# Second mlp's first product by seven block products for each pair of row tiles

## The chip, the cores and the metric

The kernel runs on one core of a Trainium2 chip. The metric is the device time of one execution in microseconds (us). Engines are named as in the profile: PE is the matrix engine (PEld its weight loads), DVE, ACT and POOL are the three elementwise engines, SP issues the DMAs. L559 is line 559 of the kernel.

## The reference, cut to what matters

```
scores  = x @ state^T / 8            # attention of 512 tokens x 32 states, 8 heads of 64
out     = concat(softmax(scores) @ state, softmax(scores^T) @ x)
x       = out as 4352 rows of 512
x       = (sigmoid(x @ w_gate) * (x @ w_val)) @ w_out        # first mlp, 512 -> 1536 -> 512
h       = x @ w_in                                           # second mlp, 512 -> 1024
s       = h * softmax(h)
y       = layernorm(s) * g_ln @ w_out2                       # 1024 -> 512
```

The changed part is `h = x @ w_in`: for a tile of 128 rows, 512 inputs in 4 blocks of 128 and 1024 outputs in two halves of 512.

## The kernel before

The 4352 rows are 8 blocks of 512 (one for each batch) and one block of 256 (the read of the state side, SREAD), that is 34 tiles of 128 rows. All wide products keep each operand as a high and a low part: `mm3` (L136 to L139) issues three matmuls, high by high (L137), low by high (L138), high by low (L139). The parts are made by a *split*: the high part by an ACT copy (`hi_of`, L128), the low part by a subtraction on DVE (`lo_of`, L134) or POOL. 

**First mlp.** Its instructions stand in program order on each engine. The blocks run one after the other, each in 12 passes (c = 0 to 11) of 24 matmuls: 6 into the bank gps (gate), 6 into the bank vps (value), 12 that add pass c-1 to the block's output in acc0 to acc3. Around them, in one pass: ACT takes the sigmoid of gps (L559, called sigma(c) below; the gate products of pass c+1 write the same bank, so they wait for it), DVE multiplies it with vps (L563), ACT and DVE split the result (gh L128, gl L569), and split the next state weights (mh L128, ml L134). In SREAD and in the last block a weight converter (`conv`) runs beside this, one step in each pass from c = 2 on: ACT L194 and L195, DVE L202, L205, L212, POOL L222 turn a 128 x 512 piece of weights from DRAM into f32, and ACT L233 and DVE L234 split the piece of the pass before. In the last block these are the pieces of w_out2, and POOL has only L222 to do.

**Second mlp.** From L995 on the order is made by a scheduler from a model of the engines, out of program order. Tile i: 2 halves by 4 k by 3 = 24 matmuls (`h2_mm`, L616 to L622), row maxima (DVE L625), exponential (ACT L632), product with h (DVE L635), layer norm (DVE L636, L637; ACT L640 applies it), then a transpose: DVE L674 by 32 x 32, a write to DRAM and four reads back (SP L675, L677), and a split of what comes back (ACT L128 into woh9, woh10, woh11 and xe2; POOL L686). 24 matmuls with w_out2 into att0 or att1 follow (`out2`, L688 to L694), and a scaled store (ACT L699, SP). Inputs of later blocks lie in DRAM, are read by `y_load` and split by `y_split` (L604 to L609: 4 ACT, 4 POOL instructions of 128 x 512 a block). Blocks come in the order 7, 0, SREAD, 1 to 6.

## Time and profile before

| | us |
|---|---|
| median of 3 runs | 1138.1 (1137.03 to 1147.5) |
| the profiled execution | 1136.54 |
| its span, first to last instruction | 1134.6 |
| PE busy in the span | 1101.0 (97%) |
| DVE, ACT, POOL busy | 691.8, 556.5, 301.7 |
| mean granted clock of PE | 0.997 of full speed |
| last block of the first mlp (12 passes) | about 685 to 752 |
| second mlp, from its first to its last first product | about 752 to 1110 |

The profiled execution is 1.56 us (0.14%) below the median. 1.94 us of it lie outside the span. The page's share of an engine is an average over stages that differ; the views by window and the timelines in the section on rows show the two stages that the change touches. In a timeline a row is start, duration, engine, line, operation, output and inputs, shapes, and in brackets how long the engine had been idle before and what ended that. Ends of matmuls are modelled.

### The profile page before, as it was taken

The numbers are of one execution on the slowest core, as the hardware profiler recorded it, in microseconds if no ns is written. First come the engines' busy times: TensorE is split into PE (matmuls) and PEld (weight loads), VectorE is DVE, ScalarE is ACT, GpSimd is POOL, SyncE is SP. The second block draws the span as 40 slices with busy tenths as digits, with TensorE's granted clock in tenths as the row PEclk, the third lists the DMA queues.
The fourth block names the chain that finished last, engine by engine and source line by source line (L and its number), as shares of the span: only waits on it lengthen the run. The fifth ranks groups of instructions, "written<-read, shape, count | busy, mean of one in ns | idle before, by whom it ended". The sixth has DMA issues, their size and how long they took to land.

```text
span 1134.6 us, 15718 instructions
## 1 busy us (share of the span) xinstructions
PE 1101.0 (97%) x5591; PEld 876.0 (77%) x5591; DVE 691.8 (61%) x1279; ACT 556.5 (49%) x1036; POOL 301.7 (27%) x301
## 2 busy tenths in 40 slices
PE   7878899999999999999999999999999999999998
PEld 5555567778878778778778998888888888888787
DVE  6999865467465475564674465758465555555462
ACT  6766445545444555443554454654453443434333
POOL 2776633300000000000000151233353443424231
PEclk9999999999999999999999999999999999999999
DMA  8763130331440421622412334424454434333331
GB/s 234 255 204 98 26 89 1 80 87 35 119 120 20 124 58 38 171 69 64 98 31 77 131 113 130 121 72 162 138 169 132 154 121 148 121 112 121 112 124 53
DMA packets 139550, 122.87 MB, mean 108 GB/s; under 512 B 70992, under 2 KB 111184, under 8 KB 139472
## 3 DMA queue, kind: packets, MB, share of 16 engines
q1 hardware_dynamic: 139472, 121.87, 36.4%
q8 instruction: 44, 0.72, 0.3%
q14 instruction: 34, 0.28, 0.1%
HBM read 78.32 MB, written 43.52 MB: 107 GB/s over the span
## 4 chain that ended last, share of the span: by engine, by line
PE 61%; DMA 13%; DVE 12%; ACT 5%; issue 4%; SPq 3%; POOL 1%; ACTq 0%; POOLq 0%; DVEq 0%
PE acc L137 9%; PE acc L139 9%; PE acc L138 9%; DMA ut<-usp 6%; DMA usp<-ub 6%; PE gps L137 4%; PE gps L138 4%; PE gps L139 4%; PE vps L137 4%; PE vps L139 4%; PE vps L138 4%; SPq L677 2%; PE att L139 2%; PE att L137 2%; PE att L138 2%
## 5 line engine op out<-in xcount | busy, mean ns | idle before, releaser
L137 PE MATMUL acc<-gh,woh 128*128 128x512 f32 (+1 forms) x432 | 168.0, 389 | 0.0
L138 PE MATMUL acc<-gl,woh 128*128 128x512 f32 (+1 forms) x432 | 164.1, 380 | 1.7 <-POOL gl L569 1.3
L139 PE MATMUL acc<-gh,wol 128*128 128x512 f32 (+1 forms) x432 | 164.0, 380 | 0.0
L563 DVE TENSOR_TENSOR sg<-vps,sg 128x512 f32<-128x512 f32 (+1 forms) x108 | 71.1, 659 | 150.5 <-PE vps L139 136.6
L559 ACT ACTIVATE sg<-gps 128x512 f32<-128x512 f32 (+1 forms) x108 | 61.8, 572 | 160.7 <-PE gps L139 156.2
L686 POOL TENSOR_TENSOR wol<-ut,woh 128x512 fp32r<-128x512 f32 x48 | 61.7, 1301 | 193.1 <-ACT woh L128 176.7
L137 PEld LDWEIGHTS acc<-gh,woh 128*128 128x128 f32 x432 | 81.5, 189 | 31.0 <-issue 15.6
L138 PEld LDWEIGHTS acc<-gl,woh 128*128 128x128 f32 x432 | 81.6, 189 | 17.7 <-POOL gl L569 2.2
L139 PEld LDWEIGHTS acc<-gh,wol 128*128 128x128 f32 x432 | 81.4, 188 | 16.0
L128 ACT ACTIVATE woh<-ut 128x512 fp32r<-128x512 f32 x48 | 28.6, 627 | 122.4 <-DMA ut<-usp 121.9
L128 ACT ACTIVATE gh<-sg 128x512 fp32r<-128x512 f32 (+1 forms) x101 | 60.5, 599 | 49.3 <-DVE sg L563 49.3
L137 PE MATMUL gps<-ah,mh 128*128 128x512 f32 x192 | 76.1, 396 | 5.2 <-DVE ml L134 4.0
L139 PE MATMUL att<-woh,wol 128*128 128x512 f32 (+1 forms) x204 | 79.5, 390 | 0.6 <-POOL wol L686 0.6
L137 PE MATMUL att<-woh,woh 128*128 128x512 f32 (+1 forms) x204 | 79.5, 390 | 0.0
L138 PE MATMUL att<-wol,woh 128*128 128x512 f32 (+1 forms) x204 | 79.1, 388 | 0.0
L134 DVE TENSOR_TENSOR ml<-gps,mh 64x512 fp32r<-64x512 f32 (+2 forms) x57 | 38.7, 678 | 63.1 <-ACT stg L128 51.0
L222 POOL TENSOR_TENSOR tt<-tt,xn 128x512 int32<-128x512 int32 x16 | 20.9, 1306 | 211.5 <-PE vps L139 153.8
L137 PE MATMUL vps<-ah,mh 128*128 128x512 f32 x192 | 75.4, 393 | 1.1 <-DVE ml L134 1.1
L138 PE MATMUL gps<-al,mh 128*128 128x512 f32 x192 | 75.6, 394 | 0.9 <-DVE al L134 0.9
L128 ACT ACTIVATE mh<-gps 64x512 fp32r<-64x512 f32 (+2 forms) x53 | 31.3, 590 | 91.6 <-PE gps L139 60.5
L139 PE MATMUL gps<-ah,ml 128*128 128x512 f32 x192 | 75.5, 393 | 0.0
L255 POOL MEMSET xtr<- 32x256 f32 x18 | 5.4, 302 | 262.2 <-PE att L323 261.5
(288 smaller groups left out, 2750.0 us busy)
## 6 DMA issues: line engine op xcount, KB each, us to landing
usp<-ub SPq DMA_DIRECT2D x32, 512.0 KB, 2.6
ut<-usp SPq DMA_DIRECT2D x128, 128.0 KB, 2.9
msp<-stg SPq DMA_DIRECT2D x72, 128.0 KB, 2.3
stg<-msp SPq DMA_DIRECT2D x36, 256.0 KB, 2.9
xn<-in_x_dram SPq DMA_DIRECT2D x15, 512.0 KB, 5.2
e2t<-in_x_dram SPq DMA_DIRECT2D x96, 64.0 KB, 2.6
stge<-in_moe_w_out_dram SPq DMA_DIRECT2D x10, 512.0 KB, 4.4
stge<-in_moe_w_gate_dram SPq DMA_DIRECT2D x9, 512.0 KB, 5.1
```

Of the source, the lines that this page charges most:

```text
L128: return act(dst, src, AF.Copy)
L134: return vec.tensor_tensor(out=dst, in0=src, in1=r(hi), op=ALU.subtract)
L137: mm(o, lh, rh, start=start, stop=False)
L138: mm(o, lh, rl, start=False, stop=False)
L139: return mm(o, ll, rh, start=False, stop=stop)
L222: pool.tensor_tensor(out=ti, in0=ti, in1=lo, op=ALU.add)
L255: pool.memset(s[:, :, 64 * (1 - i):64 * (1 - i) + 64], 0.0)
L559: act(sg[c % 2][:, 0:n], gps[:, 0:n], AF.Sigmoid)
L563: vec.tensor_tensor(out=g, in0=vps[:, 0:n], in1=g, op=ALU.mult)
L677: nc.sync.dma_start(out=w[32 * b:32 * b + 32].rearrange("p (a e) -> p a e", a=4), in_=d.rearrange("(a j) (b e) -> b j a e", a=4, b=4)[b],)
L686: pool.tensor_tensor(out=lv, in0=wv[:, 4 * q:4 * q + 4], in1=r(hv), op=ALU.subtract)
```

## The change

The 30 tiles of all blocks but the first (15 pairs) get `h` by seven products of a 128 x 256 block of x with a 256 x 512 block of w_in, in Winograd's form of Strassen's scheme. A pair has two row tiles (A1x, A2x) and two column halves of x; w_in has blocks B11 to B22. With S1 = A21 + A22, S2 = S1 - A11, S3 = A11 - A21, S4 = A12 - S2 and T1 = B12 - B11, T2 = B22 - T1, T3 = B22 - B12, T4 = B21 - T2 (`y_pair_ops`, `w_pair_ops`), `product` issues 2 x 3 matmuls for one of P1 to P7: 42 for a pair instead of 48. P6 and P7 are added onto P1 in PSUM; three ACT copies (L1116, L1121, L1123) and three DVE additions (`plus`) for each pair form the four quarters of h from them. Pairs alternate between the banks acc0, acc1, acc2 and acc3, gps, vps. The products' order is 1, 2, 5, 6, 3, 7, then out2 of tile i-2, then 4, then out2 of tile i-1.

The sums of inputs are made in `y_pair_ops`: 7 splits and 4 sums a block, 7 ACT and 11 POOL instructions instead of 4 and 4. The sums of weights are made once, in the last block of the first mlp, two steps after each pass (`w_steps`): 8 joins of high and low part, 8 differences and 8 splits, each a 128 x 512 instruction on POOL, and for each split one on ACT. Buffers are merged to make room (tt and ee are now wa, xtr and e2t wb); the out buffers are 2 instead of 4. The first block's 4 tiles are done as before, and the first mlp before its last block is as it was. The diff, cut to its core:

```diff
-    xtr = [f32t(f"xtr{i}", S) for i in range(2)]
-    tt = [f32t(f"tt{g}", S) for g in range(2)]
-    ee = [f32t(f"ee{g}", S) for g in range(2)]
-    e2t = [f32t(f"e2t{g}", S) for g in range(2)]
+    wa, wb = f32t("wa", 4, S), f32t("wb", 4, S)
+    tt, ee = [[wa[:, 2 * n + g] for g in range(2)] for n in range(2)]
+    xtr, e2t = [[wb[:, 2 * n + g] for g in range(2)] for n in range(2)]
...
-    stt = [f32t(f"stt{i}", 4, 64) for i in range(2)]
+    sttb = f32t("stt", 2, 4, 64)
+    stt = [sttb[:, i] for i in range(2)]
...
-        sbx = (ctx if p < 3 else x_late).enter_context(tc.tile_pool(name=f"sbx{p}", bufs=1, side="right"))
+        sbx = (ctx if p < 2 else x_late).enter_context(tc.tile_pool(name=f"sbx{p}", bufs=1, side="right"))
...
-    ob = sg + spill[0:2]
+    ob = sg
...
+    p1, u2 = spill[0:2]
+    p5 = sttb.rearrange("p i j n -> p (i j n)")
+    ys, ts = [], {}
+    A11, A12, A22, S1, S2, S3, S4 = range(7)
+    prod = {1: (A11, "B11"), 2: (A12, "B21"), 3: (S4, "B22"), 4: (A22, "T4"), 5: (S1, "T1"), 6: (S2, "T2"), 7: (S3, "T3")}
 
...
+    def y_pair_ops(q):
+        m = S if order[q] < B else SR
+        v = yf[q % 2][:, :, 0:m].rearrange("p (c k) (t r s) -> p c k t r s", c=2, r=2, s=P)
+        a = {(i + 1, c + 1): v[:, c, :, :, i, :] for i in range(2) for c in range(2)}
+        def split(n, src):
+            h, l = [x[:, 0:2 * (m // 2)].rearrange("p (k t s) -> p k t s", k=2, s=P) for x in ys[q % 2][n]]
+            def f():
+                hi_of(h, src)
+                pool.tensor_tensor(out=l, in0=src, in1=r(h), op=ALU.subtract)
+            return f
+        def add(dst, x, y, op):
+            return lambda: pool.tensor_tensor(out=dst, in0=x, in1=y, op=op)
+        return [
+            split(A11, a[1, 1]), split(A12, a[1, 2]), split(A22, a[2, 2]),
+            add(a[2, 2], a[2, 1], a[2, 2], ALU.add), split(S1, a[2, 2]),
+            add(a[2, 1], a[1, 1], a[2, 1], ALU.subtract), split(S3, a[2, 1]),
+            add(a[1, 1], a[2, 2], a[1, 1], ALU.subtract), split(S2, a[1, 1]),
+            add(a[1, 2], a[1, 2], a[1, 1], ALU.subtract), split(S4, a[1, 2]),
+        ]
+    def w_pair_ops(bf):
+        steps = []
+        for k in range(2):
+            b = {n: x for n, x in zip(("B11", "B12", "B21", "B22"), bf[4 * k:4 * k + 4])}
+            def join(n):
+                h, l = win(k + 2 * (n[1] == "2"), int(n[2]) - 1)
+                return lambda: pool.tensor_tensor(out=b[n], in0=r(h), in1=r(l), op=ALU.add)
+            def sub(o, x, y):
+                return lambda: pool.tensor_tensor(out=b[o], in0=b[x], in1=b[y], op=ALU.subtract)
+            def split(n, x):
+                h, l = ts[n, k]
+                def f():
+                    hi_of(h, b[x])
+                    pool.tensor_tensor(out=l, in0=b[x], in1=r(h), op=ALU.subtract)
+                return f
+            steps += [
+                join("B11"), join("B12"), sub("B11", "B12", "B11"), split("T1", "B11"),
+                join("B22"), sub("B12", "B22", "B12"), split("T3", "B12"),
+                sub("B22", "B22", "B11"), split("T2", "B22"),
+                join("B21"), sub("B21", "B21", "B22"), split("T4", "B21"),
+            ]
+        return steps
 
...
+    def banks(i):
+        return ([acc[0], acc[1], acc[2]], [acc[3], gps, vps])[i // 2 % 2]
 
     def h2_out(i, f):
-        return acc[2 * (i % 2) + f]
+        if tiles[i][0] == 0:
+            return acc[2 * (i % 2) + f]
+        a, b, c = banks(i)
+        return ((b, c), (a, p5))[i % 2][f]
+    def product(i, n, o, start, stop):
+        q, b, t = tiles[i]
+        x, w = prod[n]
+        h, l = ys[q % 2][x]
+        m = (S if b < B else SR) // 2
+        for k in range(2):
+            sl = slice(m * k + P * (t // 2), m * k + P * (t // 2) + P)
+            w1, w2 = win(k + 2 * (w[1] == "2"), int(w[2]) - 1) if w[0] == "B" else ts[w, k]
+            mm3(o, h[:, sl], l[:, sl], w1, w2, start and k == 0, stop and k == 1, skip_group_check=True)
...
+    def plus(o, x, y):
+        vec.tensor_tensor(out=o, in0=x, in1=y, op=ALU.add)
 
...
-        return (woh[9 + n], wol[9 + n]) if n < 3 else (wpart(xe, 2, 0), wpart(xo, 2, 0))
+        return (woh[9 + n], wol[9 + n]) if n < 3 else [x.rearrange("p k n -> p (k n)") for x in (sth, stl)]
...
+                x_late.close()
+                sbt = ctx.enter_context(tc.tile_pool(name="sbt", bufs=1, side="right"))
+                for w in ("T1", "T2", "T3", "T4"):
+                    for k in range(2):
+                        ts[w, k] = [sbt.tile([P, 512], F32R, name=f"{w}{e}{k}") for e in "hl"]
+                more = [[sbt.tile([P, 512], F32R, name=f"ys{i}{e}") for e in "hl"] for i in range(6)]
+                ys += [[*zip(yh[i], yl[i]), *more[3 * i:3 * i + 3]] for i in range(2)]
+                bf_pool = ExitStack()
+                sbf = bf_pool.enter_context(tc.tile_pool(name="sbf", bufs=1, side="right"))
+                w_steps = w_pair_ops([sbf.tile([P, 512], F32, name=f"bf{i}") for i in range(8)])
...
+                if last:
+                    for _ in range(2):
+                        w_steps.pop(0)()
...
+    for i in range(len(first), nt, 2):
+        q, b, t = tiles[i]
+        if t == 0 and q + 1 < len(order):
+            ops = y_pair_ops(q + 1)
+        o, v, w = banks(i)
+        end = i + 2 == nt
+        product(i, 1, o, True, False)
+        act(p1, o, AF.Copy)
+        product(i, 2, v, True, True)
+        plus(v, v, p1)
+        h_max(i, 0)
+        product(i, 5, w, True, False)
+        act(p5, w, AF.Copy)
+        product(i, 6, o, False, False)
+        act(u2, o, AF.Copy)
+        product(i, 3, w, False, True)
+        plus(w, w, u2)
+        h_max(i, 1)
+        product(i, 7, o, False, False)
+        plus(p5, o, p5)
+        h_max(i + 1, 1)
+        chain(i)
+        out2(i - 2)
+        store(i - 2)
+        if not end:
+            trans(i)
+        row_scale(i)
+        product(i, 4, o, False, True)
+        h_max(i + 1, 0)
+        chain(i + 1)
+        n = (S if b < B else SR) // P // 2
+        next_ops(q, ops, t // 2, n)
+        out2(i - 1, range(NF2 // 2) if end else range(NF2))
+        if not end:
+            store(i - 1)
+            trans(i + 1)
+            row_scale(i + 1)
+    trans(nt - 2)
+    out2(nt - 3, range(NF2 // 2, NF2))
+    store(nt - 3)
...
```

The order of instructions, at three places. First ACT in the last block of the first mlp, one pass from sigmoid to sigmoid (L559; gps is the gate's bank, woh2 a piece of w_out2, xn1 its raw words). Before:

```order
L559 ACTIVATE sg1_110<-gps_178 128x512
L128 ACTIVATE mh_93<-stg1_112 128x512
L128 ACTIVATE gh1_96<-sg1_110 128x512
L233 ACTIVATE woh2_67<-tt0_103,glnt_118 128x512
L194 ACTIVATE tt1_104<-xn1_100 128x512
L195 ACTIVATE xn1_100<-xn1_100 128x512
L559 ACTIVATE sg0_109<-gps_178 128x512
```

and with the change, in pass 5, whose split is T4's first half:

```order
L559 ACTIVATE sg1_104<-gps_171 128x512
L128 ACTIVATE mh_93<-stg1_106 128x512
L128 ACTIVATE gh1_96<-sg1_104 128x512
L233 ACTIVATE woh2_67<-wa_101,glnt_111 128x512
L194 ACTIVATE wa_101<-xn1_100 128x512
L195 ACTIVATE xn1_100<-xn1_100 128x512
L128 ACTIVATE T4h0_5304<-bf6_5329 128x512
L559 ACTIVATE sg0_103<-gps_171 128x512
```

Ahead of the next pass's sigmoid there now stands the high part of T4 (T4h0), which is read from bf6, the result of a difference on POOL. Passes 1, 3, 4, 5, 7, 9, 10 and 11 have such a row.

Second, POOL in passes 3 to 6 of the same block (L222 is the converter's addition, one for each pass). Before:

```order
L222 TENSOR_TENSOR tt0_103<-tt0_103,xn0_99 128x512
L222 TENSOR_TENSOR tt1_104<-tt1_104,xn1_100 128x512
L222 TENSOR_TENSOR tt0_103<-tt0_103,xn0_99 128x512
L222 TENSOR_TENSOR tt1_104<-tt1_104,xn1_100 128x512
```

With the change (L638 are joins, L641 differences, L648 the low parts of splits, bf4 to bf7 their buffers):

```order
L222 TENSOR_TENSOR wa_101<-wa_101,xn1_100 128x512
L648 TENSOR_TENSOR T3l0_5301<-bf5_5328,T3h0_5300 128x512
L641 TENSOR_TENSOR bf7_5330<-bf7_5330,bf4_5327 128x512
L222 TENSOR_TENSOR wa_101<-wa_101,xn0_99 128x512
L648 TENSOR_TENSOR T2l0_5297<-bf7_5330,T2h0_5296 128x512
L638 TENSOR_TENSOR bf6_5329<-xe1_1197,xo1_1198 128x512
L222 TENSOR_TENSOR wa_101<-wa_101,xn1_100 128x512
L641 TENSOR_TENSOR bf6_5329<-bf6_5329,bf7_5330 128x512
L648 TENSOR_TENSOR T4l0_5305<-bf6_5329,T4h0_5304 128x512
L222 TENSOR_TENSOR wa_101<-wa_101,xn0_99 128x512
```

Two instructions have come in behind each L222; the difference that makes bf6 stands behind the L222 of pass 5, and T4h0 above reads it.

Third, ACT in the second mlp, where a tile's exponential is L632 (now L707), the layer norm L640 (now L715), the store L699 (now L774). Before, tile by tile:

```order
L632 ACTIVATE xn0_99,stat3_128<-acc2_176,stat3_128 128x512
L632 ACTIVATE xn0_99,stat3_128<-acc3_177,stat3_128 128x512
L128 ACTIVATE woh9_74<-ut0_5802 128x512
L128 ACTIVATE woh10_75<-ut0_5802 128x512
L640 ACTIVATE xn0_99<-xn0_99,stat3_128 128x1024
L699 ACTIVATE sg1_110<-att1_181,stat1_126 128x512
```

With the change, for one pair (L1121 and L1123 are the copies of partial products; gh, ys3h, ys4h and the rows from wb the splits of the next block's inputs):

```order
L715 ACTIVATE stg1_106<-stg1_106,stat0_118 128x1024
L128 ACTIVATE gh0_95<-wb_102 128x512
L707 ACTIVATE xn0_99,stat1_119<-acc0_167,stat1_119 128x512
L707 ACTIVATE xn0_99,stat1_119<-stt_107,stat1_119 128x512
L128 ACTIVATE gh1_96<-wb_102 128x512
L1121 ACTIVATE stt_107<-vps_172 128x512
L128 ACTIVATE ys4h_5316<-wb_102 128x512
L715 ACTIVATE xn0_99<-xn0_99,stat1_119 128x1024
L128 ACTIVATE woh9_74<-ut0_5871 128x512
L128 ACTIVATE woh10_75<-ut0_5871 128x512
L128 ACTIVATE ys3h_5314<-wb_102 128x512
L774 ACTIVATE sg1_104<-att1_174,stat3_121 128x512
```

Before, the split of what came back from DRAM (woh9, woh10) stands directly ahead of the next tile's layer norm in each tile. Now in most pairs both tiles' layer norms stand ahead of the split of the first; in 5 of the 15 pairs (tiles 4 and 5, 6 and 7, 18 and 19, 22 and 23, 26 and 27) the split still stands between the two.

## Rows read from the trace of the kernel before

**Rows 1.** The page: its span, and each engine's busy us, share, instructions.

```profile
span 1134.6 us, 15718 instructions
PE 1101.0 (97%) x5591; PEld 876.0 (77%) x5591; DVE 691.8 (61%) x1279; ACT 556.5 (49%) x1036; POOL 301.7 (27%) x301
```

**Rows 2.** Windows; columns: window, its length, busy of PE, PEld, DVE, ACT, POOL.

```profile
685.00:752.00 67.00, 66.88 (x300) 55.60 (x301) 42.22 (x74) 37.28 (x65) 10.47 (x8) 1.00 0.36 105
752.00:1110.00 358.00, 357.37 (x1555) 291.48 (x1554) 201.63 (x464) 152.88 (x291) 140.13 (x159) 1.00 0.40 134
```

**Rows 3.** Waits of PE from 685 on; columns: total us, times, longest.

```profile
PE att L139 <- POOL wol L686: 0.6, 1, 0.6
```

**Rows 4.** Timeline, second mlp: first matmul of out2 in two successive tiles.

```profile
856.49 0.39 PE L137 MATMUL att<-woh,woh 128*128 128x512 f32 x1
...
867.45 0.40 PE L137 MATMUL att<-woh,woh 128*128 128x512 f32 x1
```

**Rows 5.** Timeline, last block: sigmas of passes 5, 6; first gate product of 7.

```profile
712.53 0.60 ACT L559 ACTIVATE sg<-gps 128x512 f32<-128x512 f32 x1 [0.91 <-PE gps L139]
...
717.97 0.60 ACT L559 ACTIVATE sg<-gps 128x512 f32<-128x512 f32 x1 [0.91 <-PE gps L139]
...
721.85 0.39 PE L137 MATMUL gps<-ah,mh 128*128 128x512 f32 x1
```

**Rows 6.** Lines by form, 685 to 752: count, busy us, mean ns, idle before.

```profile
L222 POOL TENSOR_TENSOR tt<-tt,xn 128x512 int32<-128x512 int32 x8 | 10.5, 1309 | 46.5 <-DVE tt L212 34.1 <-DMA xn<-in_moe_w_out_dram 12.4
...
L569 DVE TENSOR_TENSOR gl<-sg,gh 128x512 fp32r<-128x512 f32 x12 | 8.3, 692 | 3.0 <-ACT gh L128 2.1
...
L134 DVE TENSOR_TENSOR ml<-stg,mh 128x512 fp32r<-128x512 f32 x9 | 6.1, 680 | 0.0
L234 DVE SCALAR_TENSOR_TENSOR wol<-tt,glnt,woh 128x512 fp32r<-128x512 f32 x8 | 6.0, 752 | 0.0
...
L212 DVE SCALAR_TENSOR_TENSOR tt<-xn,tt 128x512 uint32<-128x512 uint32 x8 | 5.5, 692 | 0.3
...
L205 DVE TENSOR_SCALAR tt<-tt 128x512 uint32<-128x512 uint32 x8 | 3.4, 427 | 0.3
L202 DVE TENSOR_SCALAR tt<-tt 128x512 f32<-128x512 f32 x8 | 3.4, 420 | 0.0
```

**Rows 7.** Timeline, last block, pass 5: DVE's last converter step, POOL's addition.

```profile
717.55 0.69 DVE L212 SCALAR_TENSOR_TENSOR tt<-xn,tt 128x512 uint32<-128x512 uint32 x1
718.38 1.31 POOL L222 TENSOR_TENSOR tt<-tt,xn 128x512 int32<-128x512 int32 x1 [4.13 <-DMA xn<-in_moe_w_out_dram]
```

**Rows 8.** Timeline, block SREAD: DVE beside POOL.

```profile
648.62 1.30 POOL L231 TENSOR_TENSOR xo<-tt,xe 128x512 fp32r<-128x512 f32 x1 [0.74 <-ACT xe L128]
649.13 1.07 DVE L202 TENSOR_SCALAR tt<-tt 128x512 f32<-128x512 f32 x1 [0.91 <-ACT tt L194]
```

**Rows 9.** Timeline, first weights: POOL beside DVE.

```profile
70.18 1.58 POOL L222 TENSOR_TENSOR wf<-wf,stge 128x512 int32<-128x512 int32 x1
70.18 0.41 DVE L202 TENSOR_SCALAR wf<-wf 128x512 f32<-128x512 f32 x1
```

**Rows 10.** Timeline, end of the last block: table load, second mlp's first matmul.

```profile
747.98 1.28 ACT L980 ACT_TABLE_LOAD   x1
...
751.77 0.40 PE L137 MATMUL acc<-xe,mh 128*128 128x512 f32 x1
```

**Rows 11.** Timeline, second mlp: splits after the transpose, 26 tiles apart.

```profile
816.93 0.63 ACT L128 ACTIVATE woh<-ut 128x512 fp32r<-128x512 f32 x1 [1.96 <-DMA ut<-usp]
...
1109.14 0.63 ACT L128 ACTIVATE woh<-ut 128x512 fp32r<-128x512 f32 x1 [4.90 <-DMA ut<-usp]
```

**Rows 12.** Lines, 752 to 1110: POOL's low parts, DVE's product with h.

```profile
L686 POOL TENSOR_TENSOR wol<-ut,woh 128x512 fp32r<-128x512 f32 x48 | 61.7, 1301 | 193.1 <-ACT woh L128 176.7 <-PE acc L139 16.4
...
L635 DVE TENSOR_TENSOR xn<-acc,xn 128x512 f32<-128x512 f32 x44 | 29.6, 688 | 16.2 <-ACT xn L632 16.2
```

48 lines of the change are left out of this document (24 added, 24 removed).

## The prediction

> **What bounds the kernel now.** I read the page first: PE is busy for 1101.0 of 1134.6 us, no other engine for more than 61% [rows 1]. That is an average, so next the windows of the two stages that the change touches: PE is busy 66.88 of 67 us in the last block of the first mlp and 357.37 of 358 in the second mlp [rows 2]. There is hardly any idle time on PE to win; what can be won is matmuls, and what can be lost is PE's lack of waits. The view of PE's waits has one of 0.6 us as its longest after 685 [rows 3]. So I ask of each part of the change: how many matmuls go, and does anything else get so late that PE must wait for it? The timelines of the two stages answer the second question.
>
> The sum is made against the profiled execution, 1136.5 us, which lies 1.6 us (0.14%) below the median of 1138.1. About 1% of this kernel's time, 11.4 us, is what a measurement can tell from no change.
>
> **1. The matmuls removed.** In the second mlp the first matmul of out2 stands at 856.49 and, one tile later, at 867.45 [rows 4]: 10.96 us for 48 matmuls, 0.2283 each. A pair needs 42 instead of 48 for h. 15 pairs x 6 x 0.2283 = **20.6 us** less, since PE is full there [rows 2].
>
> **2. The weights' sums in the last block.** This is the term that decides. A pass lasts 5.44 us (sigma at 712.53 and 717.97 [rows 5]). POOL now has one addition of 1.31 in a pass; it gets three instructions of that kind, 3.93. By itself that fits. But DVE and POOL get in each other's way: beside a POOL instruction that lasts from 648.62 to 649.92, a DVE L202 takes 1.07 instead of its usual 0.42 and ends at 650.20, as if it had started 0.14 before POOL's end [rows 6, 8]. It works the other way too: POOL's L222 takes 1.58 instead of 1.31 beside an L202 that ends at 70.59, so it started in effect at 70.45 [rows 6, 9]. DVE's instructions in a pass that read two SBUF operands or are of L202's kind are L134, L569, L234, L202, L205, L212: 0.68 + 0.69 + 0.75 + 0.42 + 0.43 + 0.69 = 3.66 [rows 6]. If these six and POOL's three take turns, a pass needs 3.66 + 3.93 = 7.59 less 0.14 for each change of turn, more than 5.44. So work queues up, and the order decides who suffers: on ACT the split's high part (T4h0) stands ahead of the next sigma, it waits for a difference on POOL, that stands behind L222, and L222 waits for DVE's L212. And the gate product of the next pass waits for sigma.
>
> I walk through it by turns (the waiting engine starts 0.14 before the other's end, 0.15 from one engine's end to the next engine's start), in times of the trace of before. Pass 2: its L222 delays L134 and L569 of pass 3 by one POOL instruction each, because a join and a difference follow it; L212 of pass 3 ends at 709.5 instead of 707.4. Pass 3's L222 709.7 to 711.0, T3's low part 711.4 to 712.7, the difference for T2 713.1 to 714.4; DVE's rows come in between, and L212 of pass 4 ends at 716.55 instead of 712.80. T2's high part waits for that difference; sigma(5) starts at 715.2 instead of 712.53, which its 2.7 us of slack (end of sigma 718.57 to product 721.85, 3.3, less 0.15 [rows 5]) still cover. Pass 4's L222 716.7 to 718.0, T2's low part to 719.7, the join to 721.4; L212 of pass 5 ends at 723.6 instead of 718.24 [rows 7]. Pass 5's L222 723.7 to 725.05, the difference to 726.4, T4h0 726.5 to 727.1, **sigma(6) 727.1 to 727.7**. The gate product of pass 7 is wanted at 721.85 [rows 5], so PE stands still for **6.0 us**. In that time POOL and DVE catch up; the second half of the sums starts over, with T1h1 ahead of sigma(8), and by the same steps pass 9 is 5.1 late. Passes 9 to 11 hold three splits, but no converter step after 9: 0.65 at pass 11 and 4.35 until the last gh and gl are there. Last, T4's second high part and the table load of 1.28 [rows 10] stand ahead of the first conversion of the block's output: 1.3. Sum 6.0 + 5.1 + 0.65 + 4.35 + 1.3 = **17.4 us**.
>
> The ends: if no turn is taken at all, the same walk leaves only the chain L222, difference, high part, sigma: 0.95 + 2.8 + 2.25 = 6.0. If the waiting engine may not start before the other's end, it comes to 20.9. I take 17.4 since rows 8 and 9 show the turns with their 0.14.
>
> The Trainium skill ("SBUF — State Buffer", section "Who interferes with whom") says that DVE and GpSimd share one pair of ports as an exclusive lock: a DVE instruction with two SBUF inputs, or in a 2-port mode, and a GpSimd instruction that reads SBUF block each other fully, for the whole instruction. The rows agree on the turns, but show the next one begin 0.14 before the other's end. To its letter the sum would be 20.9 here and 1138.8 in all, against 17.4 and 1135.3 by the rows.
>
> **3. What the second mlp gets instead.** For a pair, three ACT copies from PSUM (0.60 each, as L559, which also reads PSUM [rows 5]) and three DVE additions (0.69, as L635 [rows 12]): 1.8 and 2.1 us of a pair's 21.92 - 1.37 = 20.55. ACT is busy 152.88 and DVE 201.63 of 358 [rows 2], so both fit. POOL gets 7 more instructions of 1.30 [rows 12] a block: 140.13 + 8 x 9.1 = 213 of about 340, 63%. Each copy has at least one product (6 x 0.228 = 1.4 us) of PE's order between it and the next product that writes or needs its bank, in most cases several or an out2 of 24. The cover holds; were it gone, a copy and its addition would cost up to 1.3 a pair.
>
> What can bind is ACT's order. Before, splits after the transpose stand 292.2 us apart over 26 tiles [rows 11], 11.24 each, while PE took 10.96: the layer norm of a tile stands behind the split of the tile before, and so each tile is one hop (layer norm, transpose, write, reads, split). PE's lead shrank by 26 x 0.28 = 7.3 and the only wait at its end is 0.6 [rows 3], so the lead had been some 6.7. With the change PE needs 20.55 for a pair, less than two hops (22.5). But in ten pairs both layer norms stand ahead of the first split, so that a pair is only one hop; in five it is two, and each of these eats some 2.0 to 2.5. The longest run of such pairs is two, 5.0, inside a lead of 6.7. Ends: 0, and 10 if the lead is gone by then (5 pairs x 2.0). I take **2**.
>
> **4. The rest.** The first block's tiles and the last three out2 stay; the merged buffers wait for readers that are done earlier on the same engines; two out buffers instead of four wait for a store two tiles before, over 20 us: 0. If a store took that long, its 0.67 on ACT would be late, hidden in the lead of 6.7.
>
> **Sum.** 1136.5 - 20.6 + 17.4 + 2 = **1135.3**, so 1135.
>
> **Rivals.**
> - *Faster: the last block keeps its cover.* POOL's extra instructions fall into DVE's pauses, and only the chain costs 6.0: 1136.5 - 20.6 + 6.0 = 1122. For it: DVE is idle 37% of that window [rows 2]. Against: the turns in rows 8 and 9, and L212 directly ahead of L222 in each pass. 0.22.
> - *Slower: the hop binds in the pair form too.* If the second tile's layer norm waits in effect for the first tile's split (its exponential waits for P4, which comes after out2 of tile i-2, and that for a split), every tile is a hop: 30 x 11.24 = 337.2, less the lead of 6.7, 330.5, against 30 x 10.96 = 328.8 before, so +1.7 in place of -20.6. 1136.5 + 1.7 + 17.4 = 1155.6. It decides from the point where most pairs are two hops; the order shows 5 of 15. 0.12.
> - *The matmuls go, but their time stays:* additions in mid-bank and copies hold PE by 1.37 us a pair. 1136.5 + 17.4 + 2 = 1156. PE's full order between copy and reuse speaks against it. 0.04.
>
> The forecast itself has 0.62: from 1128 to 1147 with its ends. Range: the low end is rival 1, 1121; the high end 1136.5 - 20.6 + 20.9 + 10 = 1147. That leaves out rivals 2 and 3 and little more. Below 1126.7 lies most of rival 1 and the low edge of the forecast: 0.24. Above 1149.5 lie rivals 2 and 3 and a remainder of 0.01: 0.17. Between, 0.59.
>
> **What would show it.** In the last block: waits of PE's gate product for sigma of 4 to 7 us in passes 7 and 9; DVE rows L134, L569, L234 of 1.3 to 2 us beside POOL; POOL busy about 42 us instead of 10.47; the second mlp's first matmul about 17 us later than 751.77 [rows 10]. In the second mlp: pairs 20.55 apart, PE's waits there few. If the first matmul comes less than 8 us later, rival 1 holds; if pairs are 22.4 apart and PE waits for the split's rows, rival 2. The prediction fails if the turns are not what sets POOL's pace, or if a bank of a pair is freed late, which would show as PE waiting for L1116, L1121, L1123 or for an addition.

## The result, and the profile after

The changed kernel takes 1151.3 us in the median (1148.3 to 1154.7, 8 runs), the kernel before 1137.0 (1134.8 to 1147.5, 8 runs): ratio 1.0116, 95% interval 1.0087 to 1.0145. It is slower by 1.2%, where 1135 and no change were forecast; the range ended at 1147.

The first two lines of the page of the changed kernel, to be held against [rows 1]:

```profile
span 1153.0 us, 15715 instructions
PE 1096.5 (95%) x5501; PEld 865.2 (75%) x5501; DVE 757.8 (66%) x1324; ACT 596.7 (52%) x1113; POOL 405.1 (35%) x381
```

90 matmuls fewer, as counted (15 x 6), but PE is busy only 4.5 us less, and idle for 23 us more. POOL has 103 us more, which its 80 new instructions of 1.3 account for. DVE has 66 us more. Only 31 of these are its 45 new instructions of 0.69; the other 35 are old instructions that take longer. Where this lies is seen in the windows of the two stages, cut at the last block's first sigma, at the second mlp's first matmul and at the end (columns as in [rows 2]):

```profile
694.28:773.48 79.20, 70.42 (x294) 56.66 (x293) 54.67 (x71) 41.20 (x72) 43.08 (x31) 0.94 0.27 79
773.48:1153.00 379.52, 363.24 (x1582) 292.03 (x1582) 259.04 (x526) 198.34 (x376) 211.63 (x220) 0.99 0.39 129
```

In the trace of before these two take 65.12 and 382.83 us. So the last block lost 14.1, where 17.4 were forecast, and the second mlp gained 3.3, where 18.6 were. The second mlp would take 382.83 - 20.55 = 362.3 if nothing waited; 17 us of the matmuls' gain were lost there. PE's waits from the second mlp's first matmul on (columns as in [rows 3]):

```profile
PE att L137 <- ACT woh L128: 9.5, 9, 2.6
PE att L137 <- ACT sg L774: 1.5, 1, 1.5
PE acc L137 <- ACT stg L1123: 1.0, 2, 0.7
PE acc L137 <- ACT stg L1116: 0.5, 2, 0.3
```

There are nine waits of out2 for the split of what came back from DRAM, 9.5 us in all; before, the second mlp had two waits for such splits, of 0.63 and 0.45.

This execution also lost 6.7 us at its start: the first sigma of the program is at 34.2 us instead of 27.4. The profiled execution of a second run (f1 below) did not, and has it at 27.5; the windows from 10 to 30 us, first of this execution, then of the second:

```profile
10.00:30.00 20.00, 17.72 (x91) 12.46 (x91) 12.65 (x25) 9.65 (x16) 3.80 (x4) 0.57 0.88 229
```

```profile
10.00:30.00 20.00, 14.39 (x112) 9.39 (x111) 17.71 (x34) 14.84 (x26) 6.55 (x6) 1.00 0.93 242
```

At a granted clock of 0.57, 91 matmuls were done where the other did 112. Of the other profiles, f3's started like that too (33.6), all others between 27.4 and 30.6, so it is no part of the change. Without it the account of f1's span (1147.6) against that of before (1134.6) reads: 0.1 to the first sigma, 1.6 from there to the last block, 14.1 in it, -2.9 in the second mlp, together 12.9.

**The last block.** The walk of the prediction can be read off in the timeline of passes 4 to 6 of the changed kernel (columns as in [rows 5]):

```profile
724.86 1.78 DVE L569 TENSOR_TENSOR gl<-sg,gh 128x512 fp32r<-128x512 f32 x1
...
726.05 1.74 POOL L638 TENSOR_TENSOR bf<-xe,xo 128x512 f32<-128x512 f32 x1
726.56 1.77 DVE L234 SCALAR_TENSOR_TENSOR wol<-wa,glnt,woh 128x512 fp32r<-128x512 f32 x1
...
730.00 1.28 POOL L222 TENSOR_TENSOR wa<-wa,xn 128x512 int32<-128x512 int32 x1 [2.21 <-issue]
731.23 1.26 POOL L641 TENSOR_TENSOR bf<-bf,bf 128x512 f32<-128x512 f32 x1
732.53 0.63 ACT L128 ACTIVATE T4h<-bf 128x512 fp32r<-128x512 f32 x1 [6.26 <-POOL bf L641]
733.06 0.58 ACT L559 ACTIVATE sg<-gps 128x512 f32<-128x512 f32 x1
...
733.70 0.80 PE L137 MATMUL gps<-ah,mh 128*128 128x512 f32 x1 [4.04 <-ACT sg L559]
```

DVE's L569 and L234 take 1.78 and 1.77 instead of 0.69 and 0.75 [rows 6] beside POOL's 1.74. L222, the difference, the high part of T4, sigma(6) and PE's gate product follow each other as in the prediction. PE waits 4.04 us instead of 6.0. But the first matmul after it takes 0.80 instead of 0.39, and the window of these 7 us of the changed kernel shows why (the number behind POOL's count is the granted clock):

```profile
732.00:739.00 7.00, 5.30 (x13) 4.24 (x14) 4.28 (x7) 5.12 (x9) 2.61 (x3) 0.52 0.36 112
```

0.52 is close to the lower of the two levels (1.2 of 2.4 GHz). PE had stood idle for 4 us before. The low level also follows the waits of 2.1 and 0.75 at the block's end, for 3.4 us; it does not follow the wait of 1.8 at 749.0. The waits in the block sum up to 8.6 us, and its 294 matmuls take 70.4 us of PE's time instead of 65.1. Waits and low clock together are 13.9 of the 14.1.

**The second mlp.** Tiles 26 and 27 of the changed kernel on ACT; the first row is the split of tile 26, the second the layer norm of tile 27, the third the split of tile 27:

```profile
1076.79 1.15 ACT L128 ACTIVATE woh<-ut 128x512 fp32r<-128x512 f32 x2 [6.07 <-DMA ut<-usp]
1078.89 1.15 ACT L715 ACTIVATE xn<-xn,stat 128x1024 f32<-128x1024 f32 x1
...
1088.56 0.63 ACT L128 ACTIVATE woh<-ut 128x512 fp32r<-128x512 f32 x1 [3.12 <-DMA ut<-usp]
```

ACT stood idle for 6 us in front of the split of tile 26, while the layer norm of tile 27, whose statistics were ready at 1073.0, stood behind it: 5.9 us lost for tile 27. PE waits 1.22 for the first split, whose own layer norm had not been held up, and 0.25 for the second. How far a split starts ahead of its out2 tells what a tile has to spare: in the changed kernel it is 2.4 to 3.9 us in tiles 0 to 3, and 0.7, which the split itself needs, in tiles 4 to 8, 19 to 24, 26, 27 and 30.

The other thing that changed is DVE's two small products of the row scale (L725 and L726, [128 x 1], L650 and L651 before, where they took 0.209 and 0.221 on average) in the view of lines of the changed kernel (columns as in [rows 6]):

```profile
L726 DVE TENSOR_TENSOR stat<-stat 128x1 f32<-128x1 f32 x33 | 18.5, 561 | 1.0
L725 DVE TENSOR_TENSOR stat<-stat 128x1 f32<-128x1 f32 x33 | 17.5, 532 | 0.8
```

That is 22 us more on DVE for the same 66 instructions (window 774 to 1130). They have two SBUF operands each and take turns with POOL, whose instructions are 128 x 512. The Trainium skill ("SBUF — State Buffer", section "Who interferes with whom") has the lock held for the whole instruction, and says that the order of issue and not the shape of the operation decides who is blocked. The trace agrees: 0.53 and 0.56 on average for products of one column. In single cases below a DVE product was held up through several POOL instructions, not one. This is the place in the second mlp where I had not applied the turns.

### The profile page after: what moved, and what is told of

Same layout as the page of the kernel before. It is cut to its first block, busy times and chain, and to the rows that moved or that the text cites. A ratio compares the mean times of both kernels' runs of the same rounds, so it can differ in the third digit from the quotient of the medians.

```text
span 1153.0 us, 15715 instructions
## 1 busy us (share of the span) xinstructions
PE 1096.5 (95%) x5501; PEld 865.2 (75%) x5501; DVE 757.8 (66%) x1324; ACT 596.7 (52%) x1113; POOL 405.1 (35%) x381
## 4 chain that ended last, share of the span: by engine, by line
PE 53%; DVE 19%; DMA 12%; ACT 5%; issue 5%; POOL 4%; SPq 2%; ACTq 0%; POOLq 0%; DVEq 0%
PE acc L137 7%; PE acc L139 7%; PE acc L138 7%; DMA ut<-usp 6%; DMA usp<-ub 4%; PE gps L137 4%; PE gps L138 4%; PE gps L139 4%; PE vps L137 4%; PE vps L138 3%; PE vps L139 3%; DVE ub L749 2%; SPq L752 2%; DVE wf L212 2%; PE att L137 2%
## 5 line engine op out<-in xcount | busy, mean ns | idle before, releaser
L563 DVE TENSOR_TENSOR sg<-vps,sg 128x512 f32<-128x512 f32 (+1 forms) x108 | 71.2, 659 | 148.6 <-PE vps L139 124.6
L559 ACT ACTIVATE sg<-gps 128x512 f32<-128x512 f32 (+1 forms) x108 | 61.5, 570 | 152.9 <-PE gps L139 148.4
L255 POOL MEMSET wb<- 32x256 f32 x18 | 5.4, 303 | 262.1 <-PE att L323 261.5
L222 POOL TENSOR_TENSOR wa<-wa,xn 128x512 int32<-128x512 int32 x16 | 20.8, 1302 | 190.6 <-PE vps L139 153.7
L569 DVE TENSOR_TENSOR gl<-sg,gh 128x512 fp32r<-128x512 f32 (+1 forms) x97 | 75.1, 774 | 10.2 <-ACT gh L128 6.9
L134 DVE TENSOR_TENSOR ml<-gps,mh 64x512 fp32r<-64x512 f32 (+2 forms) x57 | 38.7, 679 | 63.5 <-ACT stg L128 50.9
L139 PE MATMUL att<-woh,wol 128*128 128x512 f32 (+1 forms) x204 | 79.2, 389 | 0.2 <-POOL wol L761 0.2
```

The source lines that it names most:

```text
L134: return vec.tensor_tensor(out=dst, in0=src, in1=r(hi), op=ALU.subtract)
L139: return mm(o, ll, rh, start=False, stop=stop, **kw)
L559: act(sg[c % 2][:, 0:n], gps[:, 0:n], AF.Sigmoid)
L563: vec.tensor_tensor(out=g, in0=vps[:, 0:n], in1=g, op=ALU.mult)
L569: eng.tensor_tensor(out=gl[c % 2][:, 0:n], in0=sg[c % 2][:, 0:n], in1=r(gh[c % 2][:, 0:n]), op=ALU.subtract)
```

## The experiments

The order of the second mlp is a scheduler's, and it came out differently with nearly each edit: it stayed as it was, but for one or two instructions, only in f1 and g1 (against the change) and in k1 and k2 (against e3). In e1, e4, f4 and g2 a part of the arithmetic is left out or doubled, so that h is not the reference's. Each run is read by stages, from its own trace: *last block*, from its first sigma to the second mlp's first matmul (before: 65.1), and *second mlp*, from there to the end (before: 382.8; 362.3 without any loss). *Split between norms* counts the pairs, of 15, in which the first tile's split stands ahead of the second tile's layer norm on ACT. A stage is read from one execution, which lies between 4.2 us below (e2) and 7.4 us above (f3, 6.2 of them at its start) the median of its run; differences of 3 us between stages of two runs are therefore weak.

| run | median (us) | ratio to before, 95% | last block | second mlp | split between norms |
|---|---|---|---|---|---|
| the change | 1151.3 | 1.0116 (1.0087 to 1.0145) | 79.2 | 379.5 | 5 |
| f1, the change again | 1151.5 | 1.0131 (1.0102 to 1.0160) | 79.3 | 380.0 | 5 |
| e1, no weight sums | 1133.0 | 0.9944 (0.9924 to 0.9964) | 65.1 | 378.7 | 3 |
| e2, splits later | 1137.2 | 0.9992 (0.9975 to 1.0009) | 73.8 | 370.0 | 5 |
| e3, norm first | 1134.4 | 0.9971 (0.9955 to 0.9987) | 79.1 | 366.6 | 0 |
| e4, six more | 1161.0 | 1.0191 (1.0168 to 1.0214) | 79.1 | 393.8 | 6 |
| f2, e2 and e3 | 1144.6 | 1.0063 (1.0043 to 1.0082) | 73.7 | 382.6 | 0 |
| f3, e3, sums on DVE | 1134.2 | 0.9975 (0.9954 to 0.9997) | 65.1 | 382.1 | 0 |
| f4, e3, no input sums | 1129.8 | 0.9933 (0.9916 to 0.9950) | 79.4 | 361.1 | 0 |
| g1, row scale | 1141.6 | 1.0019 (1.0004 to 1.0034) | 79.2 | 372.5 | 5 |
| g2, no input sums | 1147.5 | 1.0071 (1.0045 to 1.0096) | 79.2 | 378.2 | 5 |
| g3, f3 and g1 | 1123.8 | 0.9864 (0.9839 to 0.9888) | 65.1 | 373.1 | 0 |
| h1, g3, input sums on DVE | 1130.0 | 0.9946 (0.9925 to 0.9967) | 65.1 | 376.3 | 0 |
| k1, g3 in e3's order | 1124.1 | 0.9871 (0.9851 to 0.9891) | 67.4 | 363.2 | 0 |
| k2, e3 and g1 | 1133.2 | 0.9945 (0.9921 to 0.9970) | 79.0 | 367.1 | 0 |

**e1.** The weights' sums are left out.

```diff
-                        ts[w, k] = [sbt.tile([P, 512], F32R, name=f"{w}{e}{k}") for e in "hl"]
+                        ts[w, k] = win(k + 2 * (w in ("T2", "T3")), w in ("T1", "T3"))
...
-                if last:
-                    for _ in range(2):
-                        w_steps.pop(0)()
```

> Leaves out the weights' sums: the 24 steps in the last block of the first mlp are not issued, and the products that want T1 to T4 take parts of w_in instead, so h is not the reference's. Theory (the 24 steps cost 14.1 us in the last block, by turns with DVE and by the high parts ahead of the sigmoids): first to last sigma of the last block 58.6 us as before the change instead of 71.4, the granted clock stays 1.00 there, the second mlp begins about 14 us earlier, total 1137 (1134 to 1139; the scheduler's order has 3 pairs with the split between the two layer norms instead of 5, which may give 1 to 2 more). Rival (the sums are mostly hidden, and the time is lost in the second mlp, whose tiles then start earlier and wait longer): total 1145 or more.

The last block is back at 65.14 us, clock 1.00: the sums cost the 14.1. The total came 4 us lower than expected: against f1's profiled execution 14.1 us are saved in the last block, 1.1 ahead of it and 1.2 in the second mlp, and f1's median lies 2.3 above that execution. The second mlp stayed at 378.7, although only 3 pairs have the split between the norms: the count alone does not tell its time. Part of the time stands in one place. The product with h (L710) of a quarter of h that lies in SBUF (stt) has two SBUF operands, and here it lasts through five POOL instructions in a row:

```profile
851.14 6.59 DVE L710 TENSOR_TENSOR xn<-stt,xn 128x512 f32<-128x512 f32 x1
...
857.82 0.60 ACT L1118 ACTIVATE stt<-vps 128x512 f32<-128x512 f32 x1 [4.97 <-DVE xn L710]
...
858.47 0.79 PE L137 MATMUL vps<-xe,ys5h 128*128 128x512 f32 x1 [2.94 <-ACT stt L1118]
```

The copy of the next partial product into that buffer waits for it, PE waits 2.94 us for the copy, and the clock is at its lower level for 6.8 us, which costs 3.4 more: 6 of the 16 us that this second mlp loses.

**e2.** Each split of a weights' sum is put off to the end of the next pass.

```diff
+                    late, kept = kept, []
+                    for f in late:
+                        f()
                     for _ in range(2):
-                        w_steps.pop(0)()
+                        g = w_steps.pop(0)
+                        if g.__name__ == "f":
+                            kept.append(g)
+                        else:
+                            g()
...
+        for f in kept:
+            f()
```

> Same arithmetic; each split of a weights' sum is issued one pass later (behind the converter step of the next pass, the last ones behind the first conversions of the second mlp's inputs), so that its high part on ACT no longer waits for a difference of its own pass ahead of the next sigma. Theory (what PE waits for is the high part ahead of sigma): the waits of gate products for sigma, 4.0 and 1.8 us, go, and the last block takes about 61 to 64 us from first to last sigma instead of 71.4; total 1143 (1140 to 1146). Rival (the turns between DVE and POOL take DVE's own time, 7.6 us of work for a pass of 5.4, whatever the order on ACT): the sigmoids are late all the same, through DVE's product or the split of gh; 68 us or more, total 1148 to 1151.

The result lies between the two: from first to last sigma 67.05, so ACT's order makes 4 to 5 us of the loss and DVE's own lateness the rest. No gate product waits for sigma any more. What PE waits for is now DVE (its L134, L563 and L569, 6.3 us in all), and the clock stays at 1.00; no wait is longer than 1.3. The total gained more than that: the second mlp, in another order, is shorter by 9.5, and this profiled execution lies 4.2 below its median.

**e3.** In each pair the second layer norm is issued ahead of the first split.

```diff
-            trans(i)
+            trans(i, 0)
...
-        chain(i + 1)
+        norm = chain(i + 1)
+        if not end:
+            with tc.issue_after(norm.ins):
+                trans(i, 1)
```

Here `trans(i, 0)` is the transpose, the write and the reads, and `trans(i, 1)` is the split.

> Same arithmetic; in each pair the layer norm of the second tile is issued on ACT ahead of the split of the first tile (in 5 of 15 pairs it was behind). Theory (the second mlp loses 17 us, 13 of them as waits of PE, because a tile's chain from exponential to split, about 17 us, has only 3.5 to 4.4 us to spare, and the five pairs spend 4 to 5.5 of it by the layer norm waiting for the split): waits of out2 for the split 9.5 -> 3 to 5, with the clock's share 8 us less, total 1143 (1140 to 1146). Rival (DVE and POOL, which has 7 more instructions a block, delay the chains by their turns, and the order on ACT only shows it): waits stay at 8 or more, total 1148 to 1151.

The second mlp falls by 13 us, more than expected, and the rival as it was stated, a total of 1148 or more, is out; PE's waits are 7.3 us, 1.8 of them ahead of the stage's first matmul. The edit did more than move the five splits: PE's order differs at some 50 places too. So the 13 us are the worth of this whole order. Tiles 26 and 27 on ACT in this kernel, the layer norm of 27, the splits of 26 and of 27:

```profile
1059.66 1.14 ACT L715 ACTIVATE xn<-xn,stat 128x1024 f32<-128x1024 f32 x1
1060.70 1.14 ACT L128 ACTIVATE woh<-ut 128x512 fp32r<-128x512 f32 x2
...
1069.37 0.63 ACT L128 ACTIVATE woh<-ut 128x512 fp32r<-128x512 f32 x1 [1.97 <-DMA ut<-usp]
```

From tile 27's first exponential (1054.91) to its split it is 14.5 us here; in the changed kernel (1069.24 to 1088.56) 19.3. PE does not wait at either split. The split now stands 2 us or more ahead of its out2 in 25 of the 32 tiles, instead of 14.

**e4.** P4 is issued twice, so a pair has 48 matmuls.

```diff
+        product(i, 4, o, False, False)
         product(i, 4, o, False, True)
```

> P4 is added twice, so each pair has its 48 matmuls again (h is not the reference's). Theory (the second mlp is bound by the chain of a tile, with PE waiting 13 us and some 4 of low clock): the 20.6 us of matmuls fill most of these waits, total 1151 + 4 to 8 = 1155 to 1159. Rival (the waits come from single late instructions that more matmuls do not cover): total 1168 to 1172.

It takes 9.7 us more than the change, between the two: with the old number of matmuls 11 us are lost against before, where 17 were lost. A chain that is slower than PE throughout would have left less. Single late instructions that more matmuls cover only in part would fit, but this run has another order too (6 pairs), so that is not shown.

**f1.** No edit.

> The changed kernel once more, beside the others. Theory (the first sigma of the whole kernel at 34.2 us in its first profile, 6.7 later than in five other profiles, was that one execution's): first sigma at 27 to 28.5, last block 79 us from its first sigma to the second mlp's first matmul, second mlp 378 to 380, total 1148 to 1151. Rival (the lost start belongs to the change's buffers): first sigma again at 33 or later, total 1151 to 1155.

First sigma at 27.5 and the same stages, as expected; the median lies 0.5 above the range.

**f2.** e2 and e3 together.

> Both edits of the earlier runs together: splits of the weights' sums one pass later, and in each pair the second layer norm ahead of the first split. Theory (the two stages add up): last block 73.8 us as with the later splits alone, second mlp 366.6 as with the norm first alone, total 1134.4 - 5.2 = 1129 (1127 to 1132). Rival (the second mlp's waits come from wherever the scheduler puts single instructions, so that each new order has its own): second mlp 370 or more, total 1133 or more.

The rival held: the last block adds up (73.7), the second mlp does not (382.6). With the splits at the block's end moved, the scheduler wrote another order. PE waits 2.4 and 3.0 us for the splits of tiles 12 and 13 and 2.9 near the end, and the clock falls after them. The splits of tiles 12 and 13 start 14.6 and 16.7 us after their layer norms, where e3 has 9.9 and 10.8; f3, with almost this order, shows why. The same edit that came with 13 us less in the second mlp on the change came with 12.6 us more there on e2 (7 by the medians).

**f3.** The weights' sums on DVE, ahead of the converter's step.

```diff
-                return lambda: pool.tensor_tensor(out=b[n], in0=r(h), in1=r(l), op=ALU.add)
+                return lambda: vec.tensor_tensor(out=b[n], in0=r(h), in1=r(l), op=ALU.add)
...
+                    for _ in range(1 if 1 < c < 10 else 4):
```

The low parts of the splits go to DVE as well, and each split comes one pass later, as in e2.

> Norm first, and the weights' 24 sums on DVE instead of POOL, 4 steps in passes 0, 1, 10, 11, one in the passes between, ahead of the converter's step, each split one pass later. Theory (the last block's loss is the turns between DVE and POOL; DVE by itself has 4.35 + 0.69 = 5.04 us of work in a pass of 5.44, 2.06 + 2.76 = 4.82 in the others): 59 to 61 us from first to last sigma, 66 to 68 to the second mlp's first matmul instead of 79; total 1122 (1120 to 1125). Rival (DVE is too full to take them, and what was POOL's lateness becomes DVE's): 72 us or more to the first matmul, total 1128 or more.

The last block is at 65.14 us, in the windows' view of this kernel:

```profile
692.52:757.66 65.14, 65.14 (x295) 54.17 (x293) 57.50 (x91) 40.76 (x70) 10.48 (x8) 1.00 0.34 101
757.66:1139.80 382.14, 364.97 (x1583) 293.47 (x1581) 258.00 (x528) 199.35 (x378) 213.43 (x220) 0.98 0.40 128
```

DVE is busy 57.5 us instead of 40.9, and PE does not wait once. With POOL back at its 10.5 us the turns with it are gone, and so are the 14.1 us. The run moved three things: the engine, each split by one pass (e2 alone: 5.4 us), and the number of steps in a pass; the last was not tried with the sums on POOL. The second mlp has f2's order, nearly, and f2's time, so the total is 9 above the range although the last block is in it. In front of the late splits of tiles 12 and 13 stands this, on DVE, with both tiles' layer norms (ACT) ended at 897.7 and 899.8:

```profile
896.56 1.06 DVE L725 TENSOR_TENSOR stat<-stat 128x1 f32<-128x1 f32 x1
897.67 1.22 DVE L726 TENSOR_TENSOR stat<-stat 128x1 f32<-128x1 f32 x1
898.81 1.33 DVE L725 TENSOR_TENSOR stat<-stat 128x1 f32<-128x1 f32 x1
900.18 1.22 DVE L726 TENSOR_TENSOR stat<-stat 128x1 f32<-128x1 f32 x1
901.51 1.25 DVE L750 STREAM_TRANSPOSE ub<-xn 128x1024 f32<-128x1024 f32 x1
```

Four products of 128 x 1 take 4.8 us instead of some 0.8, one POOL instruction after the other, and the first transpose comes 3.8 us after its layer norm.

**f4.** e3, without the four sums of inputs for each block.

> Norm first, and the four sums of inputs per block are left out (the splits stay, 7 per block, of unsummed parts; h is not the reference's). Theory (with the norm first, what is left of the second mlp's waits, some 5 us, comes partly from DVE's turns with POOL's added instructions): PE's waits in the second mlp 2 to 3 instead of 7.3, second mlp 363 to 365 instead of 366.6, total 1131 to 1133. Rival (the sums fall into DVE's pauses): no change, total 1134 to 1135.

The second mlp takes 361.1 us with 1.1 us of waits, so it loses nothing. That is more than expected, but it is not the price of the sums: this run's order is not e3's (POOL has 32 instructions less, and PE's order differs at some 40 places), and k1 below, in e3's order and with the sums on POOL, takes 363.2.

**g1.** The change with the row scale's two products in one instruction.

```diff
-        vec.tensor_tensor(out=s[:, 7:8], in0=s[:, 5:6], in1=s[:, 6:7], op=ALU.mult)
-        vec.tensor_tensor(out=s[:, 7:8], in0=s[:, 7:8], in1=s[:, 6:7], op=ALU.mult)
+        vec.tensor_scalar(out=s[:, 7:8], in0=s[:, 5:6], scalar1=s[:, 6:7], scalar2=s[:, 6:7], op0=ALU.mult, op1=ALU.mult)
```

> The changed kernel, with one edit: the row scale's two products of 128 x 1 on DVE, each with two SBUF operands (L725, L726, 0.53 and 0.56 us on average where they took 0.21 before the change), become one tensor_scalar with two per-row scalars, the form of L723, which keeps its 0.20 in both traces. The order of splits and layer norms on ACT is the same as in the changed kernel. Theory (POOL's added instructions hold up these small DVE instructions by a turn of 1.1 to 1.3 us each, and the next transposes and maxima behind them, which uses up the tiles' slack): PE's waits in the second mlp 12 -> 3 to 6 us, second mlp 380 -> 365 to 370, total 1151.5 -> 1137 to 1142. Rival (the order on ACT, five pairs with the split between the two layer norms, makes the waits by itself): second mlp 376 or more, total 1147 or more.

The new instruction is not held up, as its line shows:

```profile
L725 DVE TENSOR_SCALAR stat<-stat 128x1 f32<-128x1 f32 x34 | 9.2, 271 | 0.8
```

With the order unchanged on every engine, but for one ACT instruction, the second mlp falls by 7 us. The total is within the expectation; the stage is 2.5 us short of it, with 8.9 us of waits where 3 to 6 were expected. This is the cleanest comparison in the second mlp: the turns of these two products make some 7 of the 17, and the other 10 are still there.

**g2.** The change without the sums of inputs.

> The changed kernel without the four sums of inputs per block (splits of unsummed parts instead; h is not the reference's), five pairs still with the split between the layer norms. Theory (order and turns add up: with the sums gone, the five pairs alone still cost something, 2 as predicted to 8): second mlp 364 to 370 instead of 380, total 1135 to 1142. Rival (the order alone decides): 376 or more, total 1147 or more.

The result is 378.2, with 5 such pairs, as the rival had it. But they are other pairs, in another order, so neither this run nor f4 separates the sums from the order: without the sums one order costs 16 and the other nothing.

**g3.** e3, f3 and g1 together.

> Three edits together: weights' sums on DVE with splits one pass later, second layer norm ahead of the first split in each pair, row scale as one tensor_scalar. Theory: last block 65.1 us from its first sigma to the second mlp's first matmul, as before the change; second mlp 362 to 366; total 1114 to 1120, 1.6 to 2% below the kernel before. Rival (with f3's order of the second mlp, whose two late splits have another cause than the row scale): second mlp 374 or more, total 1126 or more.

It is 1.4% below the kernel before, interval 1.1 to 1.6%, but 4 us above the range. The second mlp, in nearly f3's order, is 9 us shorter than f3's with the row scale, and two of PE's waits, of 3.0 and 2.5 us, remain at late splits: the rival's cause, at a time between the two.

**h1.** g3, the input sums on DVE.

> All three edits and one more: the four sums of inputs per block go from POOL to DVE (0.7 us each there, without turns), so that POOL keeps only splits. On ACT all 15 pairs have both layer norms ahead of the first split and no split of a second tile ahead of that of the first. Theory (the second mlp's waits come from turns with POOL and from the order on ACT, and both are gone): PE's waits in the second mlp 1 to 3 us, second mlp 361 to 365, last block 65.1, total 1113 to 1117. Rival (DVE, at about 70% in the second mlp, delays the tiles' chains when it also takes the sums): second mlp 370 or more, total 1121 or more.

The rival held: the order of splits and norms is regular, and the second mlp still takes 376.3. PE waits 9.5 us for splits again. On DVE the sums take turns with POOL's splits, 0.96 us on average instead of 0.69 for those on wb, and they stand in the queue that also holds the tiles' own steps on DVE:

```profile
L620 DVE TENSOR_TENSOR wb<-wb 128x512 f32<-128x512 f32 x16 | 15.3, 958 | 2.0 <-POOL gl L616 2.0
```

**k1 and k2.** k1 is g3 with the last splits ahead of the Exp table load, which gives every engine e3's order again, but for two matmuls; k2 is e3 with the row scale alone, in the same order.

> Norm first, row scale as one tensor_scalar, weights' sums on DVE with the splits of the last pass ahead of the Exp table load, which gives ACT and PE in the second mlp the same order, instruction by instruction, as in the kernel with the norm first alone. Theory (the order that the scheduler writes decides, not the edit as such): second mlp 361 to 365, last block 65 to 67, total 1114 to 1119. Rival (an earlier start of the second mlp, or DVE's load, brings the waits back): second mlp 371 or more, total 1122 or more.

> Norm first and row scale as one tensor_scalar, weights' sums as in the change; ACT and PE in the same order as with the norm first alone. Theory (turns cost something in the good order too): second mlp 362 to 364.5 instead of 366.6, total 1130 to 1132.5. Rival (in the good order the turns fall into slack): 366 to 367, total 1134 to 1135.

The windows of k1:

```profile
689.26:756.67 67.41, 65.28 (x294) 53.96 (x293) 58.34 (x93) 41.57 (x72) 10.48 (x8) 1.00 0.33 98
756.67:1119.90 363.23, 357.95 (x1582) 293.27 (x1582) 233.51 (x492) 201.78 (x376) 212.37 (x220) 0.99 0.41 135
```

The second mlp is as the theory has it, within 1 us of its bound of 362.3; the last block is 0.4 above. The median, 1124.1, is 5 us above the theory and by its total in the rival's range: it is 2.3 above the profiled execution (1121.7), which itself lost 3 at its start (first sigma at 30.6).

k2 lands nearer to its rival, 367.1 against e3's 366.6, but not for the rival's reason. k1 and k2 have the same order in the second mlp and differ by 3.8 us. Up to 96 us after the stage's start k2 is 0.2 ahead. They part at one instruction, the product with h from SBUF again. First k1, then k2, with POOL's instructions beside it:

```profile
853.06 0.71 DVE L710 TENSOR_TENSOR xn<-stt,xn 128x512 f32<-128x512 f32 x1
853.16 1.76 POOL L616 TENSOR_TENSOR ys5l<-wb,ys5h 128x512 fp32r<-128x512 f32 x1
```

```profile
863.18 5.72 DVE L710 TENSOR_TENSOR xn<-stt,xn 128x512 f32<-128x512 f32 x1
863.31 1.28 POOL L616 TENSOR_TENSOR ys5l<-wb,ys5h 128x512 fp32r<-128x512 f32 x1
864.56 1.29 POOL L763 TENSOR_TENSOR wol<-ut,woh 128x512 fp32r<-128x512 f32 x1
865.81 1.29 POOL L763 TENSOR_TENSOR stl<-ut,sth 128x512 fp32r<-128x512 f32 x1
867.07 1.28 POOL L620 TENSOR_TENSOR wa<-wa 128x512 f32<-128x512 f32 x1
```

In k1 DVE goes first and POOL loses 0.5. In k2 POOL goes first, and DVE is held up through four of its instructions in a row, not one; three of PE's waits follow (0.22, 1.39 and 1.06 us), 2.7 of the 3.8. So a turn can cost time in the good order too, and k2 does not show that the row scale is worth nothing there: what it gave was lost again at one instruction. By the medians of their runs, each against its own runs of before, k2 is 3 us below e3, within the intervals.

## Why the prediction was wrong, step by step

- **The matmuls (20.6).** Right: k1, with all sums in place, shows the second mlp at 363.2 where 362.3 was the bound, and f4 at 361.1.
- **The last block (17.4).** The mechanism was right, step by step: e1 shows that the sums cost the 14.1, and f3 that they cost nothing on DVE. That 14.1 came near 17.4 is in part luck. The waits are 4.0 and 1.8 in passes 7 and 9 instead of 6.0 and 5.1, 2.8 instead of 4.35 for the last gh and gl, and none where 0.65 and 1.3 stood: 8.6 in all, half of the forecast. Another 5.3 us, which I had not counted, come from the low clock after them.
- **The second mlp (2, ends 0 and 10): the step that failed.** It lost 17, mainly by two things that it had wrong, and the clock added to both.
  - *The lead.* I took a lead of 6.7 us, read from before, as something that PE carries through the pairs. In the trace of before it was 6.4 at tile 5. The changed kernel never had it: a split is 2.4 to 3.9 us ahead of its out2 in the first four tiles, with nothing to spare in 14 of the 28 others; even k1 has some 4 in most tiles. The five pairs cost more than the 2.0 to 2.5 that I took for each, too: the layer norms of their second tiles (5, 7, 19, 23, 27) started 3.8 to 5.9 us after their statistics. PE's waits do not all stand there: it waited 0.16 and 0.25 at tiles 7 and 27, 0.25 to 2.33 at tiles 6, 8, 20 and 21 behind such pairs, and 1.20, 1.22 and 2.56 at tiles 4, 26 and 30, whose own layer norms were not held up. e3's whole order removed 13 us of it; what the five pairs alone cost is not shown.
  - *The turns.* I counted POOL's added instructions by POOL's own load (63%), having just worked out their turns in the block before; g1 shows 7 us for two small instructions on DVE, in an unchanged order. The product with h did not enter the sum at all. One quarter of h for each pair now lies in SBUF, so that product has two SBUF operands and takes turns as well: up to 1.42 us in the changed kernel, 6.59 in e1 and 5.72 in k2, instead of 0.69. The two causes are not additive; k1, with the order and the row scale mended, loses 1.
  - *The clock.* It falls after some of the waits here too. Around those at tile 8 the changed kernel shows, with 59 matmuls in 20 us where a full window has 89:

```profile
888.64 0.59 PE L137 MATMUL att<-woh,woh 128*128 128x512 f32 x1 [2.33 <-ACT woh L128]
...
891.54 0.80 PE L137 MATMUL att<-woh,woh 128*128 128x512 f32 x1 [1.46 <-ACT sg L774]
```

```profile
880.00:900.00 20.00, 16.21 (x59) 12.28 (x58) 11.66 (x25) 10.07 (x21) 16.02 (x17) 0.83 0.48 146
```

- **The range.** Its upper end took 10 for this step, where 17 were lost. Rival 2, the hop in every pair, named the right engine and the right two instructions, at 0.12, but with a condition that was not met (most pairs instead of five). Its 1155.6 lies near the measured 1151.3 without its mechanism having been shown.

Open: how the loss of the second mlp divides between order and turns, and the rest of e1's loss. e2 ends at 370.0 with five such pairs, in its fastest execution. The orders of both differ from the others on DVE, PE and SP too; I have not taken them apart. It was not tried to move the input sums to another stage.

## What to carry to other kernels

Work that is put "beside" a saturated engine has to be counted in turns. If DVE and POOL both read SBUF there, each instruction of the one can cost the other, however small, a whole instruction of the first, and in single cases four or five. For small per-row products there is a form that was not held up here, the tensor_scalar with per-row scalars of g1; one SBUF operand is not enough in general, since the tensor_scalar of [rows 8], 128 x 512 with one, was held up. Where a queue holds both a step that waits for a transfer and a step that starts the next transfer, the order of the two is worth a test: putting the starting step first came with 13 us less in e3, but with 12.6 us more in f2, where the scheduler had written another order. So after an edit the order that comes out has to be read before the time is explained. And slack that PE shows in one loop need not be there in the next one.

## What the runs showed of the hardware

- After the waits of 4 us PE's granted clock was at 0.50 for the next 3 to 7 us (matmuls of 0.80 instead of 0.39). After waits of 1.8 to 2.9 us it sometimes was and sometimes was not: not after 1.8 at 749.0 and 2.56 at 1122.0 in the changed kernel, but after 2.55 at 1115.4 in f1. After the waits of up to 1.3 us in e2's last block it stayed at 1.00. In the last block of the change 8.6 us of waits came with 5.3 us of this.
- A DVE product of 128 x 1 with two SBUF operands took 1.06 to 1.33 us beside a row of POOL instructions of 1.3 (f3), and 0.16 without; a tensor_scalar with two per-row scalars kept 0.27 (g1).
- A DVE product of 128 x 512 with two SBUF operands, 0.69 us by itself, lasted 5.72 us through four POOL instructions in k2 and 6.59 through five in e1; in k1, in the same order as in k2, it took 0.71.
- The first 34 us of an execution can be 6 us longer (0.57 granted clock from 10 to 30 us), in single executions of kernels that otherwise start alike.
